# x in ten first transfers instead of eight, in another item order, in a spectral filter and FFN kernel

## The chip, the cores and the metric

The kernel runs on one core of one Trainium2 chip. The metric is the device time of one execution in microseconds. TensorE (PE) does the matrix products, VectorE (DVE), ScalarE (ACT) and GpSimd (POOL) the elementwise work. Transfers are issued from SyncE (SP) and from ACT; POOL issues two gathers. Each engine carries out its own list of instructions in order and waits at semaphores for the others.

## The reference

The input x has 2048 rows of 448 values. Two layers A and B are applied twice each, always as a residual on the normalised input:

```python
def _layernorm(x, axis=-1, eps=1e-5):
    m = jnp.mean(x, axis=axis, keepdims=True)
    v = jnp.var(x, axis=axis, keepdims=True)
    return (x - m) / jnp.sqrt(v + eps)
...
    def _A_ref(x, w_r, w_i):
        X = rfft2(x.astype(jnp.float32), axes=(-2, -1))
        X = X * (w_r + 1j * w_i)
        return irfft2(X, s=(S, D), axes=(-2, -1)).astype(jnp.bfloat16)

    def _B_ref(x, w1, b1, w2, b2):
        h = jnp.einsum("bsd,df->bsf", x, w1) + b1
        r = jnp.where(h > 0, h, 0)
        return jnp.einsum("bsf,fd->bsd", r * r, w2) + b2

    x = x + _A_ref(_layernorm(x), A_w_r, A_w_i)
    x = x + _B_ref(_layernorm(x), B_w1, B_b1, B_w2, B_b2)
    x = x + _A_ref(_layernorm(x), A_w_r, A_w_i)
    x = x + _B_ref(_layernorm(x), B_w1, B_b1, B_w2, B_b2)
```

A is a filter: a two-dimensional real FFT over rows and columns, a product with complex weights (2048 by 225) and the inverse. B is a feed-forward net, 448 to 1792 to 448, with a squared ReLU and two biases.

## The kernel before, in words

**Layout.** x is split into 16 row tiles: partition p holds rows 16p to 16p+15, tile t is row 16p+t, so one tile has 128 partitions of 448 values (896 bytes each, 112 KB), and two neighbouring tiles are one run of 1792 bytes in each partition. The FFTs are written as matrix products with constant matrices: FA and FI along the 448 columns, TD and G (with GN, its negated part) forward along the rows, H and TI back. J reverses the order of rows, TQ serves the second round.

**The stages of one round.** Each has a tag, and the text uses these names.
- A1: for each of the 16 tiles the mean and variance (DVE's bn_stats, L825 and L826; tiles 1, 3 and 5 on ACT, L847 and L848), the square root on ACT (L700), the reciprocal on DVE (L856), twice the mean, negated (L839), and the scaled constant Fs = FA times 1/std (ACT L717 or POOL L718). Then five matmuls (L681) for each tile: they also use a copy of half the columns in reversed order, made in pairs of tiles and called XR.0 to XR.14 after the first tile (L707 on POOL or L706 on ACT), which the trace shows under the name VT. The sums go from PSUM to the tile XA (L706 on ACT, L707 on DVE, "evacuations"). The items of tiles 0 to 5 carry the numbers A1.0 to A1.5, those of the five pairs behind them A1.6 (tiles 6 and 7) to A1.10 (tiles 14 and 15).
- TD0 and B0: the row direction of the transform. TD matmuls of XA, evacuated to the arena, then matmuls with G and GN.
- W0: the product with the weights on DVE (L735), in pieces W0.0, W0.2, W0.4 and W0.6, and a last W0.7 for the two frequency groups at the edge, whose weights (called W08 in the code) are a transfer of their own for the real and the imaginary half. The larger weights Wt come in one transfer and one gather each.
- Bi0 and TI0: back, with H and TI; AI0 adds the result to x (L1147); ln0 turns rows into columns for the net.
- h0 and o0: the net's two matrix products. With W_sb are meant W1 and W2; W1's last 64 rows (its "tail") are a transfer of their own, followed by the rows of the bias b1, which lie in the same tile and wait for it.

The second round has the same stages: A2, TD1, B1, W1, Bi1, TI1, AI1, ln1, h1, o1. Then x goes out in transfers of one tile.

**What sets the order.** The program is not issued as it is written. Each operation is an item of a scheduler (class `_Sched`, L267): the code is run through once, the items get a number in the order of the program, and a table `ORDER` (L115) says by these numbers, for each engine, in which order they stand. PSUM banks (eight) are then given out, the waits are set, and short gaps of TensorE are filled with matmuls on a tile of ones (`warm_mm`, L1415, L1416 in the trace), as many as the scheduler's own clock model wants. An engine never takes a later item because an earlier one still waits.

**The transfers at the start.** x's tiles come in pairs, by turns on SP and ACT, SP first: 0-1, 4-5, 8-9, 12-13 on SP, with FA after the first, and 2-3, 6-7, 14-15, 10-11 on ACT in the table's order. After them SP issues TD, GN, the larger part of G, W08's real half, then the weights behind the gathers, the biases, FI, J, the rest of G, W1's tail, W08's imaginary half, the larger part of H, W2, the b1 rows, TI, the rest of W1 and the rest of H.

Of the kernel before, what the change touches and what calls it, by code (L numbers as in the profile page):

```python
# [17 lines left out]
NT = 16  # L18
# [18 lines left out]
def make_constants():  # L37
# [89 lines left out]
1354""",  # L127
    "act": """
# [12 lines left out]
1310 1313 1315 1318 1320 1323 1325 1330 1328 1335 1333 1338 1340""",  # L141
    "dve": """
# [23 lines left out]
1339 1341 1346 1255 1343 1119 1349 1352 1355""",  # L166
    "pool": """
12 15 13 16 17 14 18 20 19 22 21 53 69 61 23 77 24 85 25 116 119 26 142 145 129 132 158 155""",
# [1326 lines left out]
```

## Time and profile before

| | |
|---|---|
| median of 3 runs | 266.68 us (266.57 to 267.13) |
| the profiled execution | 267.61 us |
| its span | 265.0 us |
| PE, DVE, ACT, POOL busy | 255.3, 203.7, 175.8, 14.2 us |
| granted clock | 1.00 |
| first A1 matmul, first TD matmul | 8.08, 17.25 us |
| first product of W0 on DVE | 21.63 us |
| first matmul of h0 | 49.80 us |
| first matmul after the second filter's DVE stage | 167.16 us |

The profile is one execution on the chip. Its span runs from the first to the last instruction; the execution's time is 2.6 us longer. A line of a timeline gives the start, the time the group lasts, the engine, the line of the code, the operation, what it writes and reads, the number of instructions, and in brackets how long the engine had stood idle before it and for whom it waited. A line of busy times gives a stretch of the span and how long each engine was busy in it. PE shows a matmul until its end, so that groups overlap by a fraction of a microsecond. In the timelines a DMA row on SPq or ACTq is the issue, not the transfer.

### The profile page before, as it was taken

To read this page: it belongs to the slowest core of one execution; us is meant where nothing else is said; L and a number is where in the kernel's file an instruction comes from. 1 tells how busy PE (TensorE), PEld (TensorE's weight loads), DVE (VectorE), ACT (ScalarE), POOL (GpSimd) and SP (SyncE) were. 2 spreads that over 40 slices of the span, in tenths; PEclk is the share of its full clock that TensorE was granted. 3 is DMA by queue.
4 is the path that set the end of the run, shared out by engine and by line. 5 is a ranking of instruction groups with operands and counts; after the bars stand their busy time and mean duration, and the time that the engine had idled before them with its cause. 6 is when DMAs were issued, how large, how long until landed. Compare 5 with 4: busy or idle time off the path is not lost. (4 is left out here: it accounts for less than half of the span.)

```text
span 265.0 us, 5678 instructions
## 1 busy us (share of the span) xinstructions
PE 255.3 (96%) x2127; PEld 160.4 (61%) x2127; DVE 203.7 (77%) x653; ACT 175.8 (66%) x380; POOL 14.2 (5%) x32
## 2 busy tenths in 40 slices
PE   6999989999999999999999998899999999999996
PEld 2786678787544554455567775788654475554454
DVE  3988998999978973779996999899974239832552
ACT  5987898987549448793326988899645886311830
POOL 8840000000000000000000000000000000000000
PEclk9999999999999999999999999999999999999999
DMA  7999700023300223000000000020341000033022
GB/s 224 388 279 342 254 0 2 0 42 71 74 2 0 43 40 66 17 0 2 0 1 2 2 0 2 0 41 5 64 92 37 5 0 2 0 89 97 18 76 82
DMA packets 25531, 16.33 MB, mean 62 GB/s; under 512 B 18174, under 2 KB 24542, under 8 KB 25504
## 3 DMA queue, kind: packets, MB, share of 16 engines
q1 hardware_dynamic: 24768, 14.25, 20.4%
q10 hardware_dynamic: 576, 0.92, 1.0%
q0 software_dynamic: 160, 0.81, 0.7%
q8 instruction: 17, 0.28, 0.4%
q14 instruction: 10, 0.08, 0.1%
HBM read 10.46 MB, written 1.84 MB: 46 GB/s over the span
## 5 line engine op out<-in xcount | busy, mean ns | idle before, releaser
L681 PE MATMUL ps<-yT,W_sb 64*128 64x512 bf16 (+1 forms) x770 | 90.4, 346 | 0.0
L681 PE MATMUL ps<-W_sb,arena 128*128 128x448 bf16 (+3 forms) x476 | 87.1, 342 | 0.0
L681 PEld LDWEIGHTS ps<-yT,W_sb 64*128 64x128 bf16 (+1 forms) x770 | 52.6, 95 | 34.2 <-ACT arena L700 1.3
L735 DVE TENSOR_TENSOR arena<-arena 128x512 bf16<-128x512 bf16 (+1 forms) x140 | 44.8, 366 | 31.0 <-ACT arena L700 30.6
L681 PEld LDWEIGHTS ps<-W_sb,arena 128*128 128x128 bf16 x476 | 45.3, 98 | 38.3 <-DVE arena L735 1.5
L700 ACT ACTIVATE arena<-ps,b1col 128x512 bf16<-128x512 f32 x84 | 52.2, 688 | 24.5 <-PE ps L681 24.4
L706 ACT ACTIVATE arena<-ps 128x448 bf16<-128x448 f32 (+1 forms) x40 | 26.0, 717 | 5.5 <-PE ps L681 5.2
L700 ACT ACTIVATE mv<-mv,epst 128x1 f32<-128x1 f32 (+1 forms) x45 | 12.8, 294 | 14.7 <-DVE mv L826 13.4
L1171 ACT ACTIVATE VT<-x_sb 128x448 bf16<-128x448 bf16 x29 | 16.8, 582 | 5.5 <-DVE x_sb L1147 5.5
L700 ACT ACTIVATE arena<-ps 128x256 bf16<-128x256 f32 x56 | 17.9, 397 | 1.4 <-PE ps L681 1.1
L717 ACT ACTIVATE arena<-x_sb,rstd 128x448 bf16<-128x448 bf16 x13 | 8.8, 673 | 14.9 <-DVE rstd L1216 10.4
L706 ACT ACTIVATE XA<-ps 128x512 bf16<-128x512 f32 (+1 forms) x27 | 14.3, 581 | 4.3 <-PE ps L681 4.3
L681 PE MATMUL ps<-H_sb,arena 128*128 128x256 bf16 x128 | 15.9, 273 | 1.3 <-DVE arena L735 0.9
L681 PE MATMUL ps<-arena,G_sb 128*128 128x448 bf16 (+1 forms) x84 | 16.4, 335 | 0.2 <-ACT arena L706 0.2
L681 PE MATMUL ps<-yT,VT 64*128 64x512 bf16 x42 | 15.8, 376 | 0.0
L706 ACT ACTIVATE VT<-ps 128x1024 bf16<-128x1024 f32 (+2 forms) x20 | 14.1, 786 | 2.2 <-PE ps L681 2.1
L735 DVE TENSOR_TENSOR tmp<-arena,Wt 128x896 bf16<-128x896 bf16 x26 | 15.4, 622 | 0.1
L1293 DVE SCALAR_TENSOR_TENSOR x_sb<-ps,mv,arena 128x448 bf16<-128x448 f32 (+2 forms) x13 | 8.3, 645 | 9.3 <-PE ps L681 9.2
L681 PEld LDWEIGHTS ps<-H_sb,arena 128*128 128x128 bf16 x128 | 11.9, 98 | 4.9 <-DVE arena L735 2.9
L681 PE MATMUL ps<-TD_sb,XA 112*128 112x112 bf16 (+3 forms) x232 | 14.3, 230 | 0.3 <-DVE arena L707 0.3
L706 ACT ACTIVATE tmp<-ps 128x896 bf16<-128x896 f32 (+1 forms) x16 | 12.9, 849 | 1.5 <-PE ps L681 1.5
L681 PEld LDWEIGHTS ps<-TD_sb,XA 112*128 112x128 bf16 (+3 forms) x232 | 12.3, 103 | 2.2 <-DVE arena L707 0.5
(84 smaller groups left out, 298.5 us busy)
## 6 DMA issues: line engine op xcount, KB each, us to landing
out_dram<-x_sb SPq DMA_DIRECT2D x15, 112.0 KB, 1.8
W_sb<-in_B_w_dram SPq DMA_DIRECT2D x1, 1568.0 KB, 12.4
W_sb<-in_B_w_dram SPq DMA_DIRECT2D x1, 1344.0 KB
xin<-in_A_x_dram ACTq DMA_DIRECT2D x4, 224.0 KB, 5.5
xin<-in_A_x_dram SPq DMA_DIRECT2D x4, 224.0 KB, 7.0
H_sb<-c_H SPq DMA_DIRECT2D x1, 896.0 KB, 7.0
G_sb<-c_G SPq DMA_DIRECT2D x1, 672.0 KB, 9.5
Wt<-in_A_w_i_dram SPq DMA_DIRECT2D x1, 393.8 KB, 5.6
```

Source lines behind the costliest of these rows:

```text
L681: return sch.add("pe", lambda e: e.matmul(_res(o), lhsT, rhs, start=start, stop=stop, skip_group_check=skip), [lhsT, rhs], [o], cost=cost, ...
L700: sch.add("act", lambda e: e.activation(o, _res(i), func, **kw), rd, [o], cost=c)
L706: op = sch.add(engs[0], lambda e: e.activation(o, _res(i), ACT.Copy) if h[0].eng == "act" else e.tensor_copy(o, _res(i)), [i], [o], cost=c ...
L717: op = sch.add(engs[0], lambda e: e.activation(o, i, ACT.Copy, scale=s) if h[0].eng == "act" else e.tensor_scalar(o, i, s, 1.0, op0=ALU.mu ...
L735: sch.add(eng, lambda e: e.tensor_tensor(o, _res(a), b, op), [a, b], [o], cost=_free(o) / rate + 69.0)
L1171: op = sch.add("act", lambda e, i=i, o=o, x=x, h=h: e.activation(o, x, ACT.Square, accum_out=sd[:, i, 1:2]) if h[0].eng == "act" else e.sc ...
L1293: small(lambda e: e.scalar_tensor_tensor(out=o, in0=_res(i), scalar=rs[0] if rs else 1.0, in1=xi, op0=ALU.add if t >= 4 and last else ALU. ...
```

## The change

The first four row tiles come in transfers of one tile, the other twelve in pairs. The loop gives SP tiles 0, 1, 4-5, 8-9 and 12-13, and ACT tiles 2, 3, 6-7, 10-11 and 14-15; FA stands behind tile 1.

```diff
-        for i in range(8):
-            dma("act" if i % 2 else "sp", xin[:, 2 * i:2 * i + 2, :], x_dram[:, 2 * i:2 * i + 2, :])
-            if i == 0:
+        for i, (a, n) in enumerate([(0, 1), (2, 1), (1, 1), (3, 1)] + [(a, 2) for a in range(4, NT, 2)]):
+            dma("act" if i % 2 else "sp", xin[:, a:a + n, :], x_dram[:, a:a + n, :])
+            if i == 2:
                 dma("sp", FA_sb[:], dc["FA"])
```

There are two items more, so all later numbers are two higher, and the table `ORDER` is a new one, of the same items:

```diff
     "act": """
-5 7 11 2 9 72 56 66 57 50 58 73 100 88 74 82 103 89 106 90 113 63 93 139 79 87 126 71 108 152 118 147 121 131 134 157
...
+7 4 9 2 11 13 74 75 52 76 58 68 59 55 60 102 90 84 105 91 115 92 87 81 25 65 141 89 128 123 73 154 110 149 120 133 162
...
     "pool": """
-12 15 13 16 17 14 18 20 19 22 21 53 69 61 23 77 24 85 25 116 119 26 142 145 129 132 158 155""",
+14 18 15 16 17 19 20 21 22 79 24 71 23 63 28 26 108 118 121 95 27 144 147 131 134 160 157""",
     "sp": """
-3 6 4 8 10 28 30 29 36 32 40 41 39 31 27 34 45 37 33 47 46 38 44 35 314 334 269 352 354 355 372 390 408 426 1005 1026
...
+3 5 6 8 10 12 32 41 36 31 30 38 29 42 40 34 33 35 37 46 49 47 48 43 39 316 336 354 356 357 374 392 410 428 271 1007
...
```

In words, what moves:
- SP: tiles 0, 1, FA, 4-5, 8-9, 12-13, then GN, FI, G in both parts, TD, W08's real half, J, b2, TI, the weights behind the gathers, H in both parts, the larger part of W1, W2, W1's tail, the b1 rows, the other b1 transfer and, last, W08's imaginary half. TQ comes later among the first round's items.
- ACT: tile 3, 2, 6-7, the warming square root, 10-11, 14-15. The reversed copy XR.8 moves from POOL to ACT.
- DVE: the statistics of tiles 0 and 2 now stand around instructions that wait for ACT's square root of tile 0 and ACT's statistics of tile 3; the last ones are those of tiles 14 and 15, one of tiles 10 and 11 between them, and six statistics behind the wait for tiles 12 and 13 become five. The evacuation of b1's column goes from ACT to DVE.
- A1 to B0: TD0.0's four evacuations stand three on DVE and one on ACT (two and two before), and B0.0's two change engines. TD0.2's matmuls get another bank.
- PE: the order of tiles in A1 and of items in both filter stages; 21 matmuls on ones instead of 26, 14 of them ahead of the first A1 matmul (18 before) and three after A1.3's.

More of the change, by code (lines that the diff above doesn't have):

```diff
@@ L116 @@
     "pe": """
[10 rows of a table removed]
-1354""",
-    "act": """
[12 rows of a table removed]
-1310 1313 1315 1318 1320 1323 1325 1330 1328 1335 1333 1338 1340""",
-    "dve": """
[23 rows of a table removed]
-1339 1341 1346 1255 1343 1119 1349 1352 1355""",
[10 rows of a table added]
+1356""",
+    "act": """
[12 rows of a table added]
+1315 1317 1320 1310 1327 1325 1322 1330 1332 1337 1335 1340 1342""",
+    "dve": """
[23 rows of a table added]
+1338 1103 1336 1341 1343 1348 1307 1345 1351 1354 1357""",
     "pool": """
-12 15 13 16 17 14 18 20 19 22 21 53 69 61 23 77 24 85 25 116 119 26 142 145 129 132 158 155""",
+14 18 15 16 17 19 20 21 22 79 24 71 23 63 28 26 108 118 121 95 27 144 147 131 134 160 157""",
     "sp": """
-3 6 4 8 10 28 30 29 36 32 40 41 39 31 27 34 45 37 33 47 46 38 44 35 314 334 269 352 354 355 372 390 408 426 1005 1026
-1044 1046 1064 1047 1082 1100 1306 1303 1118 1297 1300 1206 1203 1250 1347 1259 1256 1212 1253 1350 1209 1344 1353
-1356""",
+3 5 6 8 10 12 32 41 36 31 30 38 29 42 40 34 33 35 37 46 49 47 48 43 39 316 336 354 356 357 374 392 410 428 271 1007
+1028 1046 1048 1066 1084 1049 1102 1120 1305 1205 1214 1211 1208 1255 1252 1258 1261 1308 1299 1302 1349 1352 1346
+1355 1358""",
 }
```

88 rows, old and new, of the table ORDER are left out of this document.

## The prediction

> **What bounds the kernel now.** I read the page's first two parts, then the busy time by stretches, then the chain of work that ended last, and last the timelines of single engines around the change.
>
> ```profile
> PE 255.3 (96%) x2127; PEld 160.4 (61%) x2127; DVE 203.7 (77%) x653; ACT 175.8 (66%) x380; POOL 14.2 (5%) x32
> ...
> PEclk9999999999999999999999999999999999999999
> DMA  7999700023300223000000000020341000033022
> ```
>
> TensorE is busy 255.3 of 265.0 us at a clock that stays in the top tenth, so at most 9.7 us lie open to a change that leaves the matrix work as it is. The DMA row is nearly full for the first four slices of 6.6 us and light behind: transfers can matter only in the first 33 us or so.
>
> ```profile
> 0.00:8.00 8.00, 5.61 (x18) 1.98 (x18) 3.42 (x17) 4.87 (x15) 6.76 (x17) 1.00 0.77 255
> 8.00:18.00 10.00, 9.83 (x98) 8.40 (x96) 9.08 (x40) 9.48 (x25) 7.44 (x16) 1.00 1.11 336
> 18.00:30.00 12.00, 11.69 (x98) 7.89 (x92) 10.02 (x21) 8.65 (x16) 0.00 (x0) 1.00 1.06 333
> 30.00:40.00 10.00, 9.08 (x77) 6.93 (x75) 9.93 (x19) 9.17 (x12) 0.00 (x0) 1.00 0.12 46
> 40.00:50.00 10.00, 8.76 (x107) 7.38 (x105) 8.88 (x27) 8.95 (x19) 0.00 (x0) 1.00 0.01 2
> 50.00:142.00 92.00, 92.00 (x721) 54.27 (x719) 79.42 (x306) 56.94 (x140) 0.00 (x0) 1.00 0.13 26
> ...
> 150.00:160.00 10.00, 9.65 (x104) 7.28 (x101) 10.00 (x21) 9.26 (x13) 0.00 (x0) 1.00 0.00 0
> ```
>
> The columns are stretch, length, busy time of PE, weight loads, DVE, ACT and POOL, clock, DMA share, GB/s. From 50 to 142 us TensorE has no hole at all: there an earlier start is an earlier end, and nothing else counts. Between 30 and 40 us, and again between 150 and 160, it is DVE that has no hole (9.93 and 10.00 of 10): the weight products of the two filter stages are the bound there, TensorE waits.
>
> ```profile
> 162.66 1.17 DVE arena L735 x2
> ...
> 167.16 95.54 PE ps L681 x752
> 262.70 0.02 issue
> ```
>
> The chain that ended last shows it again for the end: DVE into 167 us, then 95.54 us of matmuls without a break. So the program is a row of links: first data, A1 (PE, ACT and DVE together), the first filter on DVE, then PE, the second filter on DVE, PE. The new transfers act on the first link; the new item order can act on every one.
>
> **The head, part by part.** First the transfers.
>
> ```profile
> 4.62 0.63 DVE L825 BATCH_NORM_STATS2 st<-xin 128x6 f32<-128x448 bf16 x1 [3.77 <-DMA xin<-in_A_x_dram]
> ...
> 5.38 1.12 DVE L825 BATCH_NORM_STATS2 st<-xin 128x6 f32<-128x448 bf16 x2
> ...
> 10.42 1.16 DVE L825 BATCH_NORM_STATS2 st<-xin 128x6 f32<-128x448 bf16 x2 [0.61 <-DMA xin<-in_A_x_dram]
> ...
> 14.35 0.25 DVE L826 BATCH_NORM_AGGREGATE mv<-st 128x2 f32<-128x6 f32 x2
> ```
> ```profile
> GB/s 0 0 0 0 0 18 90 119 143 305 394 400 394 412 388 349 333 380 352 233 263 341 388 394 377 416 431 405 390 429 439 419 373 373 363 446 401 451 376 381
> ```
> ```profile
> 0.72 0.87 SPq L673 DMA_DIRECT2D xin<-in_A_x_dram  x2
> 1.64 0.42 SPq L673 DMA_DIRECT2D FA_sb<-c_FA  x1
> 2.10 1.04 SPq L673 DMA_DIRECT2D xin<-in_A_x_dram  x2
> ```
>
> The statistics start at 4.62 us, when the first transfer has landed. The second fence gives GB/s over 0 to 12 us in slices of 0.3: from 3 us on some 400 GB/s move. The first transfer of each queue shrinks from 224 to 112 KB, so 224 KB less lie ahead of the first tiles: 224 KB at 400 GB/s are 0.56 us. That is one end, 0 (landing set by latency alone) the other; I take 0.45, nearer the rate, since the bytes were moving at full rate just before the landing. Against it stand two more transfers, an issue of 0.42 to 0.45 us each on SP and ACT: everything behind the first x tiles is issued 0.45 us later, x's row tiles 12 and 13 among them, for which DVE waits at 10.42. TD, J, the gathers and the weights have to be there at 17 us and later.
>
> The Trainium skill weighs this otherwise. "DMA: Bandwidth & Descriptors", Anatomy of one DMA, gives each transfer a fixed cost of about 2 us and a variable one of bytes over 436 GB/s; by it halving one 224 KB transfer brings only about 0.26 us, an estimate, and the sum below would end 0.2 us higher. No row here separates the two parts.
>
> What of the 0.45 us reaches A1's end? DVE: in the new order it waits twice for square roots of ACT in between (tiles 0 and 3), about half a microsecond in place of the idle time gained. At 10.4 us it is bound anew by tiles 12 and 13, landing 0 to 0.45 us later; but behind them now stand five statistics where six stood (one more is done before): 0.6 us less (0.58 each in the rows). The last aggregate, ended at 14.60, ends 0.15 to 0.6 earlier. ACT takes over one reversed copy from POOL (XR.8), 448 elements:
>
> ```profile
> L847 ACT ACTIVATE arena<-xin x3: 558/560/576, 4.6 to 7.8; 128x448 bf16<-128x448 bf16 x3
> ```
> ```profile
> 14.69 0.30 ACT L700 ACTIVATE mv<-mv,epst 128x2 f32<-128x2 f32 x1
> 14.90 3.06 ACT L706 ACTIVATE XA<-ps 128x512 bf16<-128x512 f32 x6
> 19.02 0.98 ACT L706 ACTIVATE arena<-ps 128x448 bf16<-128x448 f32 x2 [1.06 <-PE ps L681]
> 21.05 3.68 ACT L706 ACTIVATE arena<-ps 128x448 bf16<-128x448 f32 x6 [1.06 <-PE ps L681]
> ```
>
> The copy costs 0.56 us, by this row of the same width. ACT is busy 9.48 of 10 us in this stretch, so most of it shows. After the last square root come six evacuations, before as in the new order, to 17.96. And TensorE, 9.83 of 10 busy, bounds the gain too: its A1 matmuls must start earlier than 8.08 by what is to be won. I take 0.3 us for A1's end, within DVE's 0.15 to 0.6; ends -0.3 (the copy whole, against the middle of DVE's gain) and +0.6.
>
> Then the step from A1 into the filter:
>
> ```profile
> 8.08 0.27 PE L681 MATMUL ps<-Fs,xin 128*128 128x256 bf16 x1
> ...
> 17.25 1.76 PE L681 MATMUL ps<-TD_sb,XA 128*64 128x224 bf16 x32
> 19.32 0.94 PE L681 MATMUL ps<-TD_sb,XA 128*128 128x224 bf16 x8 [0.31 <-DVE arena L707]
> 20.09 0.92 PE L681 MATMUL ps<-arena,G_sb 128*128 128x448 bf16 x4
> ```
> ```profile
> 21.63 0.69 DVE L735 TENSOR_TENSOR tmp<-arena 128x448 bf16<-128x448 bf16 x2 [0.33 <-ACT arena L706]
> ```
>
> The second group of eight TD matmuls waits 0.31 us for a PSUM bank that DVE empties; the G matmuls, their evacuation on ACT (21.05) and DVE's first product follow one after the other. In the new order this group gets a bank free since A1, and the first group's evacuations go three to DVE and one to ACT, all done before the G matmuls. So the wait goes whole, 0.3 us; and the evacuation for which DVE's first product waits is that of the other half, with DVE's own standing idle time of 0.33 us behind it (the row at 21.63), of which I take 0.1. Together 0.4, ends 0 and 0.6. What is late next is DVE itself, which from there to 42 us has its work in one piece; its products are the same in number.
>
> **The rest of the order.** From DVE's first product an earlier start is carried to the end, if the new order feeds DVE as closely. ACT's deliveries to the products come with margins of a few tenths, as its evacuations (0.6 us each) run back to back: I take 0.1 us as lost here, ends 0 and 0.6 (one evacuation out of turn). In the second filter the items are shuffled too: again DVE has no hole there to win (10.00 of 10), so 0, ends -0.3 and +0.3 by TensorE's single waits of 0.24 to 0.67 us around it. In the matmul stages a new order brings nothing as long as the wanted operand is there: 0. Five fewer filler matmuls (26 to 21) stood in idle time: 0.
>
> Sum against the profiled run: 265.0 of span and 2.6 around it are 267.6 us; 0.3 + 0.4 - 0.1 = 0.6 less, 267.0. The profiled run lies 0.9 above the runs' median of 266.68, so I take the difference off the median: 266.1 us.
>
> **Rivals.**
>
> *Last transfer late (slower).* The weights of the last two frequencies (W08's imaginary half) become the last transfer, behind both FFN matrices.
>
> ```profile
> 14.93 0.60 SPq L673 DMA_DIRECT2D Wt<-in_A_w_i_dram  x1
> ...
> 20.13 0.26 SPq L673 DMA_DIRECT2D W_sb<-in_B_b_dram  x1
> ...
> 21.70 2.47 SPq L673 DMA_DIRECT2D H_sb<-c_H  x1
> ```
> ```profile
> 39.04 1.16 DVE L735 TENSOR_TENSOR tmp<-arena,Wt 128x896 bf16<-128x896 bf16 x2
> ```
> ```profile
> out_dram<-x_sb SPq DMA_DIRECT2D x15, 112.0 KB, 1.8
> ```
> ```profile
> Wt<-in_A_w_i_dram SPq DMA_DIRECT2D x1, 112.5 KB, 5.4
> ```
> SP waits ahead of it, as the bias rows are issued only when the matrix's tail has landed. All transfers of before were in by 33 us, so that the wait opens at about 33; an issue of 0.6 us and a landing of 1.8 (the output's transfers, of the same 112 KB and with little beside them) put it at 35.4, against 39.04 where it is first read; its many short rows may take longer (up to the 5.4 us it took among others, 39.0). So it decides only if it lands 3.6 us later than that; then every microsecond is one of the end: 267.1 if it is one late (266.1 + 1). Chance 0.07.
>
> *ACT out of turn (slower).* DVE's two filter stages (21.6 to 42 us and the one about 150) need ACT's evacuations in the order of the products. One that comes out of turn costs DVE what one more evacuation lasts, 0.61 us (3.68 for six). It decides from the second one on: two are 1.2 us, 267.3 us. For it speaks that DVE has no hole in these stretches that would take up a late one, and ACT 9.17 of 10 busy from 30 to 40; against it that before the same engine kept DVE at 9.93 of 10. Chance 0.22.
>
> *Clock falls back (slower).*
> ```profile
> 0.98 3.86 PE L1416 MATMUL ps<-ones 128*128 128x512 bf16 x11 [0.98 <-POOL ones L748]
> 6.08 0.39 PE L1416 MATMUL ps<-ones 128*128 128x512 bf16 x1 [1.25 <-ACT mv L700]
> 6.64 1.61 PE L1416 MATMUL ps<-ones 128*128 128x512 bf16 x6 [0.16 <-DVE mv L826]
> ```
> Fillers run to 4.84, then wait 1.25 us; the granted clock stayed full. In the new order 14 stand at the head, three shorter ones behind the first real work. If the clock fell to half for 3 us around 6 to 9 us, A1's matmuls, 0.11 us apart, would lose half of 3 us: 266.1 + 1.5, 267.6 us. "TensorE: Matmul & The Clock Gate", Part 1, of the Trainium skill puts the fall after an idle window of about 3.4 us; the 1.25 us here are well under that, and the trace agrees as far as it goes. Chance 0.07.
>
> *Hidden anyway (no change).* Tiles 12 and 13 land 0.45 us later and eat what the first tiles brought, and the bank wait is replaced by the wait for ACT's evacuation. 266.7 us. Chance 0.14.
>
> **How the numbers follow.** Forecast 0.50; its own range goes from 265.2 (A1 0.6, the step into the filter 0.6, the second filter 0.3, nothing lost) to 266.7. The whole range has to reach over the slower cases, 0.36 together: 265.2 to 267.7 holds them at the prices above and leaves out about 0.15, for more evacuations out of turn and a later last transfer. A measurement of this kernel tells apart about 0.2%, 0.53 us, from no change. The forecast's 0.6 lies just beyond: of its 0.50 I give 0.41 to faster by over 0.2% and 0.09 to within. The case of no change gives 0.08 to within, 0.04 to faster, 0.02 to slower; the slower cases give 0.33 to slower and 0.03 to within. Faster 0.45, same 0.20, slower 0.35.
>
> **What would show it.** DVE's first statistic near 4.2 us; the last XA evacuation ended near 17.65; the second TD group without a wait; DVE's first product near 20.9; TensorE's unbroken stretch from about 49.2 and again 95.5 us at the end. Wrong if DVE waits for Wt at 38 to 39 us, if DVE shows holes between 21 and 42, or if matmuls of A1 stand 0.2 us apart.

## The result and the profile after

The changed kernel takes 267.79 us (median of 22 runs, 266.78 to 270.10), the kernel before beside it 266.67 us (22 runs, 266.43 to 267.36). The ratio is 1.0042, 95% interval 1.0031 to 1.0053: 1.1 us slower, where 0.6 us faster was forecast. The runs also spread over 3.3 us instead of 0.9.

The profiled execution of the changed kernel took 267.69 us with a span of 265.4, against 265.0 before. The two spans differ by only 0.4 us because the execution profiled before (267.61 us) lies above all 22 timed runs of its kernel. So the two traces show where time moves, but not the whole of its size. First the page's busy times, and stretches of the changed kernel in the columns of the prediction (stretch, length, busy time of PE, weight loads, DVE, ACT and POOL, clock, DMA share, GB/s):

```profile
PE 256.1 (97%) x2122; PEld 167.1 (63%) x2122; DVE 203.5 (77%) x655; ACT 175.0 (66%) x379; POOL 13.7 (5%) x31
```
```profile
0.00:8.00 8.00, 6.44 (x20) 2.30 (x21) 3.48 (x18) 5.18 (x16) 6.30 (x16) 1.00 0.77 242
8.00:18.00 10.00, 9.54 (x86) 7.28 (x86) 9.21 (x38) 9.36 (x25) 7.35 (x16) 1.00 1.11 341
...
30.00:40.00 10.00, 9.11 (x77) 6.88 (x75) 9.93 (x19) 8.84 (x11) 0.00 (x0) 1.00 0.09 24
...
50.00:142.00 92.00, 92.00 (x720) 61.35 (x718) 78.27 (x308) 56.81 (x139) 0.00 (x0) 1.00 0.13 26
150.00:160.00 10.00, 8.91 (x91) 5.89 (x88) 10.00 (x21) 8.17 (x13) 0.00 (x0) 1.00 0.00 0
```

The bounds are the same ones: DVE in both filters (9.93 and 10.00 of 10), TensorE in the nets, the clock full. But A1's stretch, 8 to 18 us, now has TensorE busy for 9.54 us instead of 9.83. Why, DVE's timeline of the changed kernel shows (start, time, instruction, in brackets the idle time before it and what ended it):

```profile
3.26 0.63 DVE L825 BATCH_NORM_STATS2 st<-xin 128x6 f32<-128x448 bf16 x1 [2.41 <-DMA xin<-in_A_x_dram]
...
6.39 1.15 DVE L825 BATCH_NORM_STATS2 st<-xin 128x6 f32<-128x448 bf16 x2 [0.76 <-DMA xin<-in_A_x_dram]
...
8.88 1.15 DVE L825 BATCH_NORM_STATS2 st<-xin 128x6 f32<-128x448 bf16 x2 [0.28 <-DMA xin<-in_A_x_dram]
...
11.65 1.15 DVE L825 BATCH_NORM_STATS2 st<-xin 128x6 f32<-128x448 bf16 x2 [0.52 <-DMA xin<-in_A_x_dram]
```

The first statistic starts 1.36 us earlier than before (3.26, was 4.62), but behind it DVE waits for x three times where it waited once, the last time for tiles 12 and 13, whose statistics start at 11.65 us and started at 10.42 before. The end of the program is different too. These are the last pieces of the chain of work that ended last, then TensorE's timeline at the two places that matter:

```profile
177.50 0.69 DVE x_sb L1147
...
186.60 0.09 DVE rstd L1216
186.69 0.01 issue
186.71 76.39 PE ps L681 x548
```
```profile
17.66 2.65 PE L681 MATMUL ps<-TD_sb,XA 128*64 128x224 bf16 x40
20.16 1.49 PE L681 MATMUL ps<-arena,G_sb 128*128 128x448 bf16 x7
...
179.43 7.15 PE L681 MATMUL ps<-yT,W_sb 128*128 128x256 bf16 x64
186.71 0.54 PE L681 MATMUL ps<-tmp,FI_sb 128*128 128x224 bf16 x4
187.09 5.08 PE L681 MATMUL ps<-W_sb,arena 128*128 128x448 bf16 x26
```

Before, TensorE ran unbroken from 167.16 for 95.54 us. Now the unbroken piece starts only at 186.71 and lasts 76.39 us; ahead of it, from 177.50 on, the chain runs through DVE. By stages of the two profiles (us, read from the starts of the stages' first instructions):

| stage | before | after | moved |
|---|---|---|---|
| to the last XA evacuation | 17.95 | 18.34 | +0.39 |
| from there to W0's first product | 3.68 | 3.43 | -0.25 |
| first filter, to h0 | 28.17 | 28.17 | 0 |
| first net and second A2, to TD1 | 92.21 | 92.35 | +0.14 |
| second filter, to TI1 | 25.15 | 24.83 | -0.32 |
| to h1 | 5.81 | 5.91 | +0.10 |
| h1, to o1 | 13.78 | 14.06 | +0.28 |
| o1 to the end of the last issue | 76.69 | 76.74 | +0.05 |

The sum is +0.39, as the spans have it. The step into the filter and the second filter got faster, A1 and h1 slower. The experiments take these apart, and they show that A1's row needs care: its end moves by more than 0.39 us between executions.

### The profile page after: what moved, and what is told of

Its sections match the earlier page's. It is cut to its first block, busy times and chain, and to the rows that moved or that the text cites. A ratio compares the mean times of both kernels' runs of the same rounds, so it can differ in the third digit from the quotient of the medians.

```text
span 265.4 us, 5663 instructions
## 1 busy us (share of the span) xinstructions
PE 256.1 (97%) x2122; PEld 167.1 (63%) x2122; DVE 203.5 (77%) x655; ACT 175.0 (66%) x379; POOL 13.7 (5%) x31
## 5 line engine op out<-in xcount | busy, mean ns | idle before, releaser
L681 PEld LDWEIGHTS ps<-yT,W_sb 64*128 64x128 bf16 (+1 forms) x770 | 59.2, 95 | 26.5 <-issue 0.9
L735 DVE TENSOR_TENSOR arena<-arena 128x512 bf16<-128x512 bf16 (+1 forms) x140 | 45.4, 366 | 28.4 <-ACT arena L700 28.3
L706 ACT ACTIVATE arena<-ps 128x448 bf16<-128x448 f32 (+1 forms) x38 | 25.0, 735 | 5.6 <-PE ps L681 5.4
```

Of the source, the lines that this page charges most:

```text
L681: return sch.add("pe", lambda e: e.matmul(_res(o), lhsT, rhs, start=start, stop=stop, skip_group_check=skip), [lhsT, rhs], [o], cost=cost, ...
L706: op = sch.add(engs[0], lambda e: e.activation(o, _res(i), ACT.Copy) if h[0].eng == "act" else e.tensor_copy(o, _res(i)), [i], [o], cost=c ...
L735: sch.add(eng, lambda e: e.tensor_tensor(o, _res(a), b, op), [a, b], [o], cost=_free(o) / rate + 69.0)
```

## The experiments

Every kernel here computes the whole result. "Pairs" are the eight transfers of before, "singles" the ten of the change. Times are medians; ratios stand against the kernel before on the same chip, whose median was 266.66 to 266.71 in all these comparisons.

**The parts, each alone.** The kernel before, run once more under a name of its own, bounds what a comparison can tell.

> The kernel before once more, unchanged: a second profile of it, since the first one's span (265.0 us) lies about 0.9 us above the median of its runs. Both theories expect the time of before, 266.7 us, and a span of about 264.1. If the extra 0.9 us of the first profile came from A1 (late x tiles), the first TD matmul stands before 17.25 us here; if not, it stands there again and the 0.9 us lie elsewhere.

Measured: 266.60 us (266.41 to 267.23), 0.9999 [0.9990, 1.0008]. The profiled execution was its longest again (267.23 us, span 265.2), and its first TD matmul stands at 17.46 us, 0.21 later than before. So this profile doesn't answer the question by itself. The profiles of kernels that share its first half do: there the last XA evacuation ends between 17.44 us (second filter only, an execution of 266.40 us) and 18.17 (this one), 17.95 in the first profile of before, and from there to TD1 the three agree within 0.05 us. What single executions of the old order differ by lies for the most part in A1.

Singles alone, in the order of before with the two added transfers put into it:

```diff
-        for i in range(8):
-            dma("act" if i % 2 else "sp", xin[:, 2 * i:2 * i + 2, :], x_dram[:, 2 * i:2 * i + 2, :])
+        for i, (a, n) in enumerate([(0, 1), (2, 1), (1, 1), (3, 1)] + [(a, 2) for a in range(4, NT, 2)]):
+            dma("act" if i % 2 else "sp", xin[:, a:a + n, :], x_dram[:, a:a + n, :])
```

> The four single transfers of the change, with the item order of before (the added transfers directly behind their neighbours on SP and ACT). Theory 'the order costs': the new transfers are harmless, 266.2 to 266.8 us. Theory 'the transfers cost' (x's later tiles come later and less regularly): 267.3 to 268.0 us, and DVE waits longer than 0.6 us for tiles 12 and 13 near 10.4 us.

The new order alone, with the pairs of before (the reverse of that diff, on the changed kernel):

> The new item order with the pair transfers of before. Theory 'the order costs': 267.3 to 268.2 us, as the changed kernel. Theory 'the transfers cost': 266.4 to 266.9 us.

Measured: singles alone 270.14 us (269.57 to 270.55), 1.0126 [1.0110, 1.0142]; order alone 267.32 (266.96 to 268.03), 1.0028 [1.0016, 1.0041]. So neither part is a gain. The order costs about 0.65 us by itself and the singles add 0.47 to it (267.79); the intervals of the two kernels overlap, so the 0.47 is not clear of the noise as a size. Singles in the old order cost 3.5 us, partly by another mechanism, below.

**The order, by stages.** The next kernels keep the pairs and give the new order to some stages only: everything from the second statistics' end on (TD1 to o1), the second filter only (TD1, B1, W1, Bi1), or everything from TI1 on. The diff of the last one, in the table of TensorE; the other engines' tables change alike:

```diff
     "pe": """
...
-1120 1135 1132 1102 1129 1153 1138 1016 1144 1147 1150 1156 1034 1141 1198 1171 1168 1165 1192 1186 1174 1177 1180
-1159 1054 1189 1195 1162 1183 1204 1072
...
+1120 1153 1102 1144 1129 1147 1016 1156 1150 1135 1141 1034 1138 1132 1195 1168 1159 1162 1171 1177 1165 1192 1180
+1186 1189 1174 1198 1183 1054 1204 1201
...
```

> Transfers and order of before up to the second round's statistics; from TD1 on the items in the new order. The changed kernel's trace has TensorE waiting for DVE at 186.7 us (0.3 us), in h1, where the kernel before has no wait. If the loss sits there, 267.0 to 267.2 us (0.3 to 0.5 over before); if the loss of 1.1 us sits in the first half, 266.6 to 266.8.

> The kernel before with the new order in TD1, B1, W1 and Bi1 alone (second filter). From the traces: TD1's first matmul to TI1's first takes 24.8 to 25.0 us in the new order and 25.15 in the old, so 0.2 to 0.3 us less: 266.3 to 266.5 us. Rival (the second filter's order is what makes the tail slower): 267.3 to 267.6 us.

> The kernel before with the new order from TI1 to the end alone (last step of the second filter, second net). The traces show 0.1 us more to h1, 0.2 to 0.3 us of waiting for DVE at 186.4 us and, where a transfer that transposes a tile lands 1.3 us late, another 0.5: 267.4 to 267.9 us, with a wider spread of the runs than before (its runs span 0.9 us). Rival (the loss is in the second filter): 266.6 to 266.8 us.

The reverse is the changed kernel, singles and all, with the old order from TD1 on:

> The changed kernel with the order of before from TD1 on: single transfers and the new order in the first half. If the parts add up: the changed kernel's 267.8 less the 0.85 us of the tail, 266.8 to 267.1 us. Rival (the tail's loss comes only with the disturbed first half): 267.5 to 267.9 us.

And the parts that looked good together: pairs, the new order up to Bi1, the old one from TI1 on:

> Pair transfers, the new order in the first half and in the second filter, the order of before from TI1 on. If the parts add up, both gains (0.2 to 0.3 us each) without the two losses: 266.1 to 266.4 us, faster than both kernels. Rival (the gains of the filter stages are lost again in the net behind them): 266.6 to 266.9 us.

| kernel | median, us | lowest to highest | ratio |
|---|---|---|---|
| new order from TD1 on | 267.54 | 266.89 to 267.78 | 1.0031 [1.0020, 1.0042] |
| second filter only | 266.53 | 266.34 to 266.98 | 0.9992 [0.9984, 1.0001] |
| from TI1 on | 267.18 | 266.69 to 268.84 | 1.0029 [1.0013, 1.0045] |
| singles, old order from TD1 on | 267.30 | 266.77 to 267.62 | 1.0015 [1.0004, 1.0025] |
| pairs, new order up to Bi1 | 266.27 | 266.11 to 266.43 | 0.9980 [0.9969, 0.9990] |

The last one beats both kernels, by 0.4 us against the kernel before. With it the change can be taken as a ladder: 266.7 before; 266.27 with the new order up to Bi1 and pairs; 267.32 with the new order from TI1 on as well (+1.05); 267.79 with the singles on top (+0.47). By medians the order from TI1 on costs 1.0 us behind the new second filter (267.54 less 266.53) and 0.5 behind the old one; the interval of the latter kernel reaches from 0.35 to 1.2 us, so the runs don't show that the two differ. In the profile of the quicker kernel the chain's last piece is whole, as before:

```profile
166.50 0.26 PE ps L678
166.75 0.01 issue
166.76 95.37 PE ps L678 x751
```

**What the order from TI1 on does to TensorE.** TensorE's timeline of that kernel, then of the quicker kernel with the old order there:

```profile
179.03 7.15 PE L678 MATMUL ps<-yT,W_sb 128*128 128x256 bf16 x64
186.31 0.54 PE L678 MATMUL ps<-tmp,FI_sb 128*128 128x224 bf16 x4
```
```profile
179.23 4.97 PE L678 MATMUL ps<-yT,W_sb 128*128 128x256 bf16 x44
184.04 0.55 PE L678 MATMUL ps<-tmp,FI_sb 128*128 128x224 bf16 x4
184.42 1.91 PE L678 MATMUL ps<-yT,W_sb 128*128 128x256 bf16 x16
```

With the old order 44 matmuls of h1 take 4.81 us from start to the next start, 0.1093 each. By that 64 take 7.00 us; in the new order they take 7.28. So TensorE waits 0.28 us ahead of AI1.8's four matmuls, which now stand behind the last of h1, and 0.28 is also what h1's stage is longer by. The bank that these four get is that of the h1 group two items earlier, which ACT empties last, so I moved AI1.8 ahead of those two items, into the bank before it. From TI1's first matmul to the start of TensorE's last 70 matmuls it is 84.81 us in the quicker kernel and 85.07 here, so in an execution like this one the wait is nearly the whole of what the step costs. The rest of the 1.05 follows further down.

```diff
     "pe": """
...
-1186 1189 1174 1198 1183 1054 1204 1201
...
+1186 1189 1174 1054 1198 1183 1204 1201
...
```

> The kernel before with the new order from TI1 on (267.18 us), but the matmuls at which TensorE waited at 186.3 us (AI1.8) two items earlier, where the bank they get was emptied at 185.0. Theory 'that wait for a bank, emptied late by ACT, is the loss': the wait of 0.2 us is gone, 266.8 to 267.0 us. Rival (the loss is in ACT's and DVE's order around it): 267.1 to 267.4, with a wait at another place.

Measured: 267.17 us (266.67 to 267.87), 1.0014 [1.0001, 1.0028], against 267.18 unmoved. The two intervals overlap, and the stage h1 is as long (14.06 and 14.07 us): the move brought nothing that the runs can tell. TensorE's timeline and the chain of the moved kernel show the place:

```profile
179.19 6.28 PE L678 MATMUL ps<-yT,W_sb 128*128 128x256 bf16 x56
185.59 0.54 PE L678 MATMUL ps<-tmp,FI_sb 128*128 128x224 bf16 x4
```
```profile
185.25 0.31 DVE VT L732
185.56 0.03 issue
185.59 77.26 PE ps L678 x556
```

56 matmuls would take 6.12 us, and took 6.40: again 0.28 us of waiting. The chain names DVE, whose row ends last ahead of them. But that row writes VT, and the four matmuls read tmp and FI_sb. DVE's timeline, then ACT's:

```profile
184.67 0.38 DVE L732 TENSOR_TENSOR tmp<-VT 128x448 bf16<-128x448 bf16 x1
...
185.17 0.38 DVE L732 TENSOR_TENSOR VT<-tmp 128x448 bf16<-128x448 bf16 x1
```
```profile
183.44 2.01 ACT L697 ACTIVATE arena<-ps 128x256 bf16<-128x256 f32 x7
```

DVE's last write of tmp ends at 185.05, half a microsecond too early to be the wait. ACT empties a bank until 185.45, and the four matmuls start 0.14 us later. Unmoved, ACT's emptying ends at 186.16, and they start 0.15 later, at 186.31. So the likeliest reading is that the moved matmuls got a bank again that ACT empties last, and that the move changed the bank but not the wait. To give them a bank that is long free, or to let ACT empty it earlier, was not tried.

**A transfer that stops half-way.** The kernels with the new order from TI1 on also spread more. In the pairs kernel with the new order TensorE had another wait, for the transfer that turns x's columns into rows for h1. TensorE's timeline, then the transfers from 177.2 to 179.6 us (GB/s in slices of 0.06 us, the queues, the issue and its microseconds to landing):

```profile
180.42 6.29 PE L678 MATMUL ps<-yT,W_sb 128*128 128x256 bf16 x56 [0.51 <-DMA yT<-x_sb]
```
```profile
GB/s 38 371 179 226 209 205 205 205 213 188 171 111 60 21 4 0 0 0 0 0 0 4 9 9 4 13 9 9 9 13 4 13 9 13 9 9 166 269 303 282
...
q8 instruction: 1, 0.02, 3.2%
...
yT<-x_sb SPq DMA_TRANSPOSE x1, 4.3
```

It runs at 200 GB/s, stops for about 1.2 us and then ends; a packet of the queue that loads instructions lies inside. The second run of the kernel before, at the same transfer, shows no such packet and no stop:

```profile
q1 hardware_dynamic: 1056, 0.26, 65.2%
...
yT<-x_sb SPq DMA_TRANSPOSE x1, 3.0
```

Two more single executions were taken to see how often it falls there:

> The new order from TI1 on once more, one profile: its 12 runs went from 266.69 to 268.84 us, and the first profile was one of the quick ones (267.01). If transfers that transpose a tile land late in the slower runs (4.3 us in place of 3.05, as in one earlier profile), TensorE waits for one near 180 us here when the run is over 267.3 us; if not, and the run is over 267.3, the variation sits at the start (A1's end later than 17.3 us).

> The changed kernel once more, one profile: A1's end between 17.3 and 17.9 us by the landing of x's tiles; a wait for a transposing transfer near 180 us only if an instruction fetch falls into it (its landing then 3.9 to 4.4 us after the issue in place of 3.05).

The order from TI1 on, again: 267.33 us; this transfer landed 3.96 us after its issue. The changed kernel again: 269.57 us; 4.52 us, and TensorE waited 0.69 us. Of the seven profiles with the new order from TI1 on, five have a turning transfer that landed 4.0 to 4.5 us after its issue in place of 3.0 to 3.3, and in three of them TensorE waited for it. Of ten with the old order there, one has it (4.7 us, in the kernel with singles alone). In each there is a packet of instruction loading (queue q8) in the transfer's stretch. All transposing transfers of the 17 profiles say the same: the traces tell the landing of 197, eight landed 3.7 to 4.7 us after their issue, and exactly these have a q8 packet that starts 0.7 to 2.7 us after the issue; the other 189 landed after 3.0 to 3.4. That the packet makes the stop is the likeliest reading, but it was not tried by itself; why it meets the transfer more often in the new order stays open. What it is worth shows in the stretch from TI1's first matmul to the start of TensorE's last 70 matmuls: 84.81 us in the quicker kernel, 85.05 to 85.16 in the four profiles with the new order in which this transfer didn't hold up the chain, 85.37, 85.84 and 86.03 in the three in which it did. (With the old order from TI1 on eight profiles of ten lie between 84.72 and 84.91; the kernel with singles and the old order from TD1 on has 85.05, the one with singles alone 85.70 with its late transfer.) So of the 1.05 us of the order from TI1 on some 0.3 are the wait ahead of AI1.8, and the rest comes, as far as the profiles show, in executions with a transfer that stops. How many of the timed runs were such is not on record.

**What the singles do.** The busy times from 2 to 5 us, last column GB/s: before, the pairs in the new order, the changed kernel, and its second execution.

```profile
2.00:5.00 3.00, 2.84 (x10) 0.88 (x7) 0.38 (x1) 1.87 (x3) 2.49 (x5) 1.00 0.92 313
```
```profile
2.00:5.00 3.00, 3.00 (x10) 0.95 (x7) 0.60 (x2) 1.53 (x3) 2.52 (x4) 1.00 1.01 321
```
```profile
2.00:5.00 3.00, 3.00 (x9) 1.06 (x7) 1.38 (x4) 2.82 (x7) 2.52 (x4) 1.00 0.95 256
```
```profile
2.00:5.00 3.00, 3.00 (x9) 1.06 (x7) 1.44 (x4) 2.82 (x7) 2.52 (x4) 1.00 0.92 225
```

The DMA engines show as busy, but carry less. Against this profile of the pairs 65 GB/s are missing for 3 us, 195 KB, or half a microsecond at the 390 GB/s that move afterwards. That is the size of the 0.47 us by which the singles are dearer; that it is the cause is not shown by that, as 321 is the highest of the profiles with pairs (301 to 321) and the singles lie between 216 and 256. The second execution, with 225 GB/s, shows what follows on DVE and on TensorE:

```profile
6.83 1.15 DVE L825 BATCH_NORM_STATS2 st<-xin 128x6 f32<-128x448 bf16 x2 [1.21 <-DMA xin<-in_A_x_dram]
...
9.95 1.15 DVE L825 BATCH_NORM_STATS2 st<-xin 128x6 f32<-128x448 bf16 x2 [0.90 <-DMA xin<-in_A_x_dram]
```
```profile
12.62 0.28 PE L681 MATMUL ps<-Fs,xin 128*128 128x256 bf16 x1 [0.92 <-POOL Fs L718]
```

There the first TD matmul, behind A1, starts at 18.73 us; at 17.66 in the first profile, at 17.07 with pairs in the same order. A1's end says the same with the new order in the first half: the last XA evacuation ends at 17.72, 17.78 and 17.97 us in the three profiles with eight transfers of two tiles and at 18.02, 18.34 and 19.43 in the three with the ten of the change. Three things could make the hole: shorter rows (896 bytes in place of 1792), more transfers, or smaller ones ahead. The first kernel changes the rows alone: the first two transfers are tiles 0 and 2, and 1 and 3, as many bytes as before in twice as many rows.

```diff
-            dma("act" if i % 2 else "sp", xin[:, 2 * i:2 * i + 2, :], x_dram[:, 2 * i:2 * i + 2, :])
+            s = slice(i, i + 3, 2) if i < 2 else slice(2 * i, 2 * i + 2)
+            dma("act" if i % 2 else "sp", xin[:, s, :], x_dram[:, s, :])
```

> The combination of pair transfers, the new order up to the second filter and the old order from TI1 on (266.27 us), with one thing changed: the first two transfers take tiles 0 and 2, and 1 and 3, so that their rows are 896 bytes long instead of 1792; number of transfers, issues and bytes stay. Theory 'short rows make x late': 0.3 to 0.5 us slower (266.6 to 266.8), tiles 12 and 13 land after 11 us. Rival 'the added issues make x late': 266.2 to 266.4.

The second changes the number alone: pairs, and behind the first of each queue one transfer of a single row of 896 bytes into a tile that nobody reads.

```diff
-        for i in range(8):
+        for i, (a, n) in enumerate([(0, 2), (2, 2), (0, 0), (1, 0)] + [(a, 2) for a in range(4, NT, 2)]):
...
+                dma("act" if i % 2 else "sp", junk[0:1, a, :], x_dram[0:1, a, :])
```

> The same combination with the pair transfers kept and one tiny transfer (one row of 896 bytes into an unused tile) added on each queue, behind the first pair: the issues of the changed kernel without its short rows. Theory 'the added issues make x late' (0.45 us each): 0.3 to 0.5 us slower than 266.27. Rival 'short rows': 266.2 to 266.4.

> The kernel with two tiny added transfers once more, one profile: its runs went from 266.5 to 270.6 us and its first profile was the quickest of them (A1's end 17.25 us). Theory 'x lands late, and where the fillers tied to it start late the clock falls': A1's end at 17.7 us or later, a wait of DVE for x of over 0.5 us, and in a run of over 269 us a granted clock under 1.0 near 8 us. Rival (the loss lies behind A1): A1's end near 17.25 again.

The third keeps the singles and the number of eight, with tiles 8 to 11 and 12 to 15 in one transfer each:

```diff
-        for i in range(8):
+        for i, (a, n) in enumerate([(0, 1), (2, 1), (1, 1), (3, 1), (4, 2), (6, 2), (8, 4), (12, 4)]):
```

> The combination (new order up to the second filter, old order from TI1 on) with the four single transfers of the change, but tiles 8 to 11 and 12 to 15 in one transfer each, so that each queue issues four x transfers as before and not five. Theory 'the added issues make x late': the first tiles come early and nothing behind them is later, 265.9 to 266.3 us. Rival (four small transfers at the head delay the rest by themselves): 266.7 to 267.0, as the same order with the change's ten transfers should be.

All three stand on the quicker kernel of 266.27 us. Measured: short rows 266.37 us (266.16 to 266.82), 0.9980 [0.9969, 0.9992], no difference. Two tiny transfers 267.85 (266.53 to 270.59), 1.0066 [1.0039, 1.0093]; the one execution behind it 268.75. Singles in eight transfers 267.84 (267.44 to 268.52), 1.0047 [1.0035, 1.0059]. From 2 to 5 us the kernel with short rows, then the one with singles in eight transfers:

```profile
2.00:5.00 3.00, 3.00 (x9) 1.06 (x7) 0.77 (x4) 1.76 (x4) 2.51 (x4) 1.00 0.95 301
```
```profile
2.00:5.00 3.00, 3.00 (x10) 0.98 (x7) 1.33 (x4) 2.49 (x5) 2.52 (x4) 1.00 0.88 256
```

So row length is out. The hole at 2 to 5 us comes with the small first transfers, also when there are only eight in all. A fourth reading was not tried: with small transfers ahead fewer bytes stand issued early on. By 2.1 us the two engines had issued 1184 KB before and 736 KB in the changed kernel. Against it as the only cause speaks the kernel with singles alone: 896 KB, and yet only 216 GB/s. The time of the kernel with singles in eight transfers is not a clean price, though: on ACT tile 2 was issued ahead of tile 3, unlike in the change, and DVE waited 1.08 us for the square root behind tile 3's statistics. An additional transfer, however small, costs as well, by itself and at another place: with the tiny ones 311 GB/s moved from 2 to 5 us in the single execution, but the tiles behind were late, and TensorE's timeline of it has the longest wait in A1 of all:

```profile
13.27 0.28 PE L679 MATMUL ps<-Fs,xin 128*128 128x256 bf16 x1 [1.63 <-POOL Fs L716]
```

What inside the transfer queues leaves these holes, and why they vary so much from run to run, stays open. In two of the eleven timed runs with the tiny transfers, and in one of the 22 of the changed kernel, the mean granted clock was 0.994 and the time over 270 us.

**Singles in the old order, and the clock.** Their mean granted clock was 0.994 too, in three of four runs. Busy times of the profiled one, then TensorE's and DVE's timelines:

```profile
6.00:8.00 2.00, 0.45 (x3) 0.12 (x2) 1.11 (x3) 0.62 (x4) 1.27 (x3) 1.00 1.06 385
8.00:10.00 2.00, 2.00 (x6) 0.82 (x7) 2.00 (x16) 1.88 (x8) 1.58 (x4) 0.55 1.05 423
10.00:12.00 2.00, 2.00 (x13) 1.47 (x12) 1.42 (x8) 0.70 (x2) 2.00 (x5) 0.59 1.04 384
```
```profile
7.57 1.69 PE L1414 MATMUL ps<-ones 128*128 128x512 bf16 x4 [1.53 <-DVE st L823]
```
```profile
6.89 0.63 DVE L823 BATCH_NORM_STATS2 st<-xin 128x6 f32<-128x448 bf16 x1 [2.21 <-DMA xin<-in_A_x_dram]
```

In the old order the tiles 4 and 5 are wanted first after the singles. They landed at 6.69 us, DVE waited 2.21 us, TensorE's filler matmuls waited behind DVE, and from 8 to 12 us the clock was 0.55 and 0.59. At 0.57 on average 4 us of matmuls lose about 1.7 us, of 2.3 that A1 ended later (first TD matmul at 19.58 against 17.25). The rest of the profile's loss, about one more microsecond, goes with a later turning transfer that landed 4.72 us after its issue and lies on the chain. The fourth run had the full clock and still took 269.57 us; so the clock isn't the whole price, and what that run lost instead no profile shows. Nor does the length of the idle piece alone say when the clock falls: the 1.63 us ahead of the row at 13.27, in the kernel with the tiny transfers, left it at 1.00, with TensorE busy for 0.50 us from 11 to 13 us. What made it fall here stays open; one profile shows it.

## Why the prediction was wrong

- *Bounds of before: held.* DVE in the filters and TensorE in the nets are the bound after as before, and what A1 loses is seen at the end.
- *First transfers, 0.45 us earlier: missed by a factor of three, 1.36 us, and this did not matter.* The working took the bytes ahead of the first tiles as the price. It did not ask what the flow behind does while the first small transfers run. The estimate of 0.26 us from the Trainium skill, "DMA: Bandwidth & Descriptors", Anatomy of one DMA, lies farther off still. That section gives its cost for transfers that GpSimd issues, and x is issued by SP and ACT. Of the 1.36 us no two rows here say which part is fixed cost and which is bytes; about a quarter of a microsecond of it comes without smaller transfers: with pairs in the new order the first statistic starts at 4.35 to 4.41 us, with pairs in the old one at 4.44 to 4.79.
- *Two more transfers, tiles 12 and 13 0 to 0.45 us later: the step that failed.* They landed 1.2 us later (11.65 against 10.42), and DVE waited for two pairs ahead of them too, 0.76 and 0.28 us. I had priced an added transfer by its issue alone, 0.42 to 0.45 us. The profiles show a hole in the flow besides, 216 to 256 GB/s from 2 to 5 us where pairs have 301 to 321, and in the second execution the statistics of tiles 12 and 13 start another 0.8 us later, at 12.44. Why small first transfers make the hole stays open.
- *A1's end, 0.3 us earlier: 0.39 later*, beyond the end of -0.3 that I had kept. With pairs the same order ended A1 at 17.72 to 17.97 us in three profiles, the old one at 17.44 to 18.17 in seven: a gain of the order here is not to be seen. With the singles it ended later in each of three, at 18.02 to 19.43. So the 0.3 us that were to come from the earlier first tiles did not reach A1's end, though the first statistic was 1.36 us earlier.
- *Step into the filter, 0.4 us: mechanism right, 0.25 measured.* The bank wait of 0.31 went whole: the row at 17.66 has 40 TD matmuls in one piece. But DVE's wait ahead of its first product did not shrink by 0.1, it grew from 0.33 to 0.41.
- *First filter, 0.1 lost by ACT out of turn: 0 measured.* 28.17 us in both.
- *Second filter 0, ends -0.3 and +0.3: a gain of 0.32*, just beyond that end. DVE had no hole there, but the way into its piece of products became shorter (6.18 to 6.03 us), the piece itself (17.31 to 17.24) and the way out (1.66 to 1.56). The working had no term for this; that it helps the forecast is luck.
- *Matmul stages, "a new order brings nothing: 0": the second failing step.* The condition I named, that the wanted operand is there, left out that a matmul needs a bank as well. AI1.8's matmuls wait 0.28 us behind h1 for a bank that ACT empties; 0.14 and 0.10 are lost in the first net and ahead of h1; and where the turning transfer stops, the operand is late too, and TensorE waits 0.5 to 0.7 us in some executions. By medians the order from TI1 on costs 1.05 us where the sum had 0. The step was argued from the stretch 50 to 142 us, which has no hole, and was carried over to the second round without a look at 177 to 187 us.
- *Rivals.* Last transfer late: hidden, as said; it landed at 35.09 (I said 35.4) and its product ran at 39.24 without a wait. ACT out of turn: not seen in the filters, where I looked (DVE 9.93 and 10.00 of 10); what h1 has is a bank that ACT empties late. Clock: full in the changed kernel's profile; it fell where the singles met the old order, behind an idle piece of 1.53 us, and not behind one of 1.63 us in another kernel. The 1.53 us are well short of the 3.4 us window of "TensorE: Matmul & The Clock Gate", Part 1, of the Trainium skill, on which the small chance rested; the measurement decides. None of the rivals was the one that came true: more time for the same bytes.
- *The sum.* By the ladder the pairs with the new order up to Bi1 gain 0.4 us. The stages give this as 0.25 for the step into the filter, which was forecast, and 0.32 for the second filter, which was not, less what the first net and the way to h1 lose. Against it stand 1.05 us of the order from TI1 on, forecast as 0, and 0.47 of the singles, whose earlier landing of 0.45 us was to carry A1's gain. -0.4 + 1.05 + 0.47 is the measured +1.1 by medians; the 0.47 is the least certain of the three.

## What to carry to other kernels

A smaller first transfer brings the first tile early, and its price stands at the tiles behind: look at when the last of a series lands and at the GB/s in between, not at the first landing. A new order of items is not one edit but one for each stage; tried stage by stage, this one had a gain of 0.4 us and a loss of 1 us in it. Where an instruction is moved to get rid of a wait, list all that it needs at the new place, the bank too: here it met a wait of the same 0.28 us there. And the engine that the profile names for a wait is the one that ended last; check that it writes what the waiting instruction reads. Compare a stage's length over several profiles of the same code before you explain a few tenths in it: A1 with nothing changed ended anywhere from 17.44 to 18.17 us.

## What the runs showed of the hardware

- Two transfers of 896 bytes, read by nobody, put behind the first pair cost 1.6 us in the median (267.85 against 266.27) and spread the runs over 4 us. Halving the rows of the same bytes cost nothing (266.37).
- A transfer within SBUF that transposes can stop in the middle (in the profile shown for 1.2 us, at 0 to 13 GB/s in place of 200); it then lands 3.7 to 4.7 us after its issue instead of 3.0 to 3.4. Exactly the eight of 197 that did so had a packet of instruction loading that started 0.7 to 2.7 us after their issue. That the packet is the cause was not tried by itself.
- The granted clock fell to 0.55 after a stretch in which TensorE was busy 0.45 of 2 us, its longest idle piece 1.53 us. With an idle piece of 1.25 us (before) it stayed full, and also with one of 1.63 us in a stretch with 0.50 of 2 us busy (the single execution with the tiny transfers); so neither figure is a threshold.
